# Early feed-forward weights, weight sums kept in DRAM, two-bank reads on ScalarE, and new instruction orders in a one-core transformer block

## The chip, the cores and the metric

The kernel runs on one core of one Trainium2 chip. A core has five engines with instruction streams of their own: TensorE (PE, with its weight loads listed as PEld), VectorE (DVE), ScalarE (ACT), GpSimd (POOL) and SyncE (SP), which here issues nearly all DMAs. The metric is the device time of one execution in microseconds, the median of several runs. Differences within about 1% can't be told from no change with this kernel.

## The reference

One transformer block on a sequence of 2048 tokens of width 512, in float32:

```
mod = silu(c) @ w_mod                      # six rows of 512: sa, ca, ga, sb, cb, gb
h   = layernorm(x) * (1 + ca) + sa
x   = x + ga * attention(h)
h   = layernorm(x) * (1 + cb) + sb
x   = x + gb * (relu(h @ w1 + b1)**2 @ w2 + b2)
```

The attention has 32 heads of width 16 and cuts the sequence into four segments of 512 tokens. Within a segment it is causal softmax attention; beside it each head reads a memory M, z that was summed over the segments before, with phi(t) = t + 1 for positive t and exp(t) otherwise:

```
for s in range(4):
    a_dot = softmax(q_s k_s^T / 4 + mask) v_s
    a_mem = phi(q_s) M / (phi(q_s) z + 1e-6)
    o_s   = g * a_mem + (1 - g) * a_dot      # g = sigmoid(beta), one per head
    M, z  = M + phi(k_s)^T v_s, z + sum(phi(k_s))
attention = concat(o_s) @ wo
```

The feed-forward layer is 512 to 1792 to 512 with a squared relu.

## The kernel before, in words

**Precision.** Matrix products that need float32 accuracy split each operand into a high part (a cast to a shorter float32 form) and a low part (the difference), and add three products. So each weight and each activation tile costs a cast, mostly on ScalarE, and a subtraction, mostly on VectorE.

**Stages.** A unit u is one segment (u // 4) and eight heads (u % 4); there are 16. For each unit, `qk` (L757) projects queries and keys into PSUM, ScalarE and VectorE split them into a staging tile `sg`, and twelve DMAs spread `sg` into four of the twelve slots of `ST` (`fill`, L812). `a_quad` (L863) forms scores a first time to get row maxima: TensorE at L870, maxima on VectorE at L875, a first pair of banks through a copy `ac` in SBUF (L908). The maxima go back into `ST` by DMA (L948). `b_quad` (L1032) forms the scores again with keys on the partitions (L1040), ScalarE takes the exponential (L1057), GpSimd zeroes what the mask forbids (L1044), and TensorE multiplies with the values (L1099). `vproj` (L823) projects the values, `mem` (L954) reads and updates the memory. `wo_tile` (L1222) applies wo to 128 tokens and adds x. The second layer norm and the feed-forward layer follow in four blocks of 512 tokens. Each block runs `ffn1` (L1434) seven times, q = 0 to 6, for 256 of the 1792 hidden features, and `ffn2` (L1493).

`ffn1` multiplies 2 x 2 blocks with seven products instead of eight. For that `load_w1` (L1382) makes, for each block and q, not only the four weight quarters but also four sums and differences of them (`sums`, L1404, four additions on VectorE), and splits all seven into high and low (casts at L1396, subtractions at L1399). The same sums are made again for each of the four blocks.

**Start.** x and the columns of w_mod for the first layer norm are loaded first. Matmuls without use (`N_WARM` of them, L546) keep TensorE busy from its start, reading a mask that GpSimd builds. `mod_parts` multiplies w_mod with silu(c) (L568), `mod_cols` turns the result into columns (L588), and the layer norm applies them after a transposition (L616). The first projection (`qk` of unit 0, L747) needs that and the split first columns of wq and wk. The load of wv goes into a buffer that the modulation weights of the start hold before it.

**Order.** `Plan` collects all operations as nodes with their dependences, buffers and a priority. For each engine a written list of node numbers (`ORDER`) says in which order it issues; numbers count the nodes in the order of their creation. The plan's constants (durations, `RARE`, `COLD`, `FREE`) model the engines' times; the written lists decide the order. An engine is a queue: an instruction that waits holds all behind it. SP's DMAs are issued in order too, at most eight in flight.

**Seam.** `open_ffn` (node `N_FFN`, L1371) closes the attention's SBUF buffers and opens those of the feed-forward layer: W2, w1r (raw w1, two), w1d (split w1, two), rr, r, u, gbb. `N_FFN` comes after all nodes of attention, and every load of w1 and w2 waits for it. The last four `wo_tile` calls, whose input stays in SBUF (X1L), lie behind it too.

**PSUM.** Each of the eight banks is a tile of its own (`bank`, L458), and each ScalarE read is of one bank.

Of the kernel before, what the change touches and what calls it, by code (L numbers as in the profile page):

```python
# [8 lines left out]
F32 = mybir.dt.float32  # L9
F32R = mybir.dt.float32r  # L10
# [8 lines left out]
P = 128  # L19
# [15 lines left out]
N_WARM = 70  # L35
# [35 lines left out]
1015 1106 926 1012 1018 1114 1022 1025 1002 928 1111 1142 930 1030 1034 1145 1120 1133 1038 1035-1036 1128 1045 1041
1272 1048 1363 1053 1364 1116 1365 1125 1234 1366 1242 1057-1059 1130 1148 1368 1155 1369 1151 1370 1135 1371 1163
1061 1253 1063 1167 1247 1396-1397 1239 1398-1399 1158 1266 1401-1402 1171 1403 1244 1404 1258 1168-1169 1178 1530
1181 1261 1531 1174 1532-1533 1263 1275 1186 1535-1536 1249 1537 1430 1438 1538 1468 1190-1192 1281 1413 1288 1414
1284 1415 1194 1416 1296 1196 1291 1418-1419 1268 1420 1449 1459 1443 1421 1278 1940-1941 1950-1951 1457 1435
1300-1302 1440 1304 1601 1311 1663 1314 1664 1454 1307 1665 1445 1666 1563 1471 1462 1668-1669 1319 1670 1464 1576
1671 1571 1474 1323 1582 1324-1325 1573 1796 1477 1797 1484 1798 1568 1492 1799 1487 1592 1801 1578 1802 1604 1590
1480 1803 1327 1804 1696 1329 1496 1595 1500 1497-1498 1607 1587 1507 1503 1734 1706 1510 1515 1519 1709 1610 1613
1520-1521 1617 1704 1597 1523 1620 1525 1737 1701 1625 1629 1740 1715 1633 1723 1630-1631 1640 1636 1958 1711 1959
1829 1842 1960 1834 1961 1867 1643 1963-1964 1648 1837 1965 1870 1966 1720 1652-1654 1873 1839 1743 1656 2114 1750  # L80
1658 2115-2116 1844 1728 2117 1987 1758 1988 1848 1989-1990 1725 2119 1746 1992-1993 1753 1861 1994-1995 1853
2120-2121 1730 1858 2122 2059 2021 1762-1764 1766 2034 2004 1856 2005 1769 2006 1773 2007 1776 1781 2009 2026 2010
# [1477 lines left out]
```

## Time and profile before

| | |
|---|---|
| median of 3 runs | 775.79 us (775.1 to 780.02) |
| profiled execution | 778.38 us, its span 776.7 us |
| TensorE clock granted, mean | 0.993 |
| busy: PE, PEld, DVE, ACT, POOL | 97%, 77%, 83%, 66%, 30% |
| read from HBM, written to it | 46.16 MB, 10.49 MB |
| attention's last unit ends, first ffn1 product | about 450 us, 460.46 us |

The page of the profile gives busy time per engine, the chain of work that ended last, the costliest groups of instructions and the DMA issues. Other views give the same execution by stretches of time, by wait, and in order of time. In a row of a group stand line, engine, operation, tiles out<-in, shapes and count, then busy time and the mean duration in ns, then the idle time before with what ended it. "x32" in a row in order of time merges neighbours of one line.

### The profile page before, as it was taken

How to read it: one execution, taken by the hardware profiler on the slowest of the kernel's cores; microseconds unless marked ns; L12 is line 12 of the kernel's file. 1: busy time of each engine (PE TensorE's matmuls, PEld its weight loads, DVE VectorE, ACT ScalarE, POOL GpSimd, SP SyncE). 2: the span in 40 equal slices, each digit the busy share in tenths (PEclk: the TensorE clock that was granted, in tenths of full speed). 3: DMA queues.
4: the chain of work that ended last, by engine and by line, in shares of the span. 5: the costliest groups of instructions: out<-in, count | busy, mean ns of one | idle time of the engine just before them, and what ended most of it. 6: DMA issues, size and time to landing. Idle time of an engine off the chain costs nothing.

```text
span 776.7 us, 17899 instructions
## 1 busy us (share of the span) xinstructions
PE 756.3 (97%) x6576; PEld 594.2 (77%) x6579; DVE 643.3 (83%) x1643; ACT 509.2 (66%) x990; POOL 233.6 (30%) x351
## 2 busy tenths in 40 slices
PE   8998999999999999999999989999999999999998
PEld 4777657675787858875676668888888888998896
DVE  3577877897888897789889889999989998998753
ACT  0658768879779896778756836667555665655541
POOL 3555453537665786534513310000000010000000
PEclk9999999999999999999999999999999999999999
DMA  7574661330443324244654166322351121043201
GB/s 270 174 182 107 203 182 52 89 98 23 118 124 83 98 71 103 55 116 127 167 176 132 49 201 192 96 82 82 108 174 58 41 96 55 28 136 101 63 1 54
DMA packets 78097, 84.81 MB, mean 109 GB/s; under 512 B 9014, under 2 KB 47674, under 8 KB 78011
## 3 DMA queue, kind: packets, MB, share of 16 engines
q1 hardware_dynamic: 77858, 83.55, 37.4%
q8 instruction: 52, 0.85, 0.5%
q14 instruction: 35, 0.28, 0.1%
q10 hardware_dynamic: 152, 0.13, 0.1%
HBM read 46.16 MB, written 10.49 MB: 73 GB/s over the span
## 4 chain that ended last, share of the span: by engine, by line
PE 69%; DVE 16%; ACT 6%; issue 3%; SPq 3%; DMA 2%; POOL 1%; ACTq 0%; DVEq 0%; POOLq 0%
PE bqk L757 9%; PE bpv L1099 6%; PE bpf L1502 5%; PE bpf L1504 5%; PE bpf L1503 5%; PE ba L870 5%; PE bpb L1040 5%; PE bv L837 4%; PE bhy L1443 3%; PE bhy L1444 2%; PE bhy L1445 2%; ACT pt L1057 2%; SPq L812 2%; PE bwarm L546 2%; DVE w1r L1404 2%
## 5 line engine op out<-in xcount | busy, mean ns | idle before, releaser
L875 DVE CUSTOM_DVE_ANT_0 ba<-ba,msk 128x128 f32<-128x128 f32 (+2 forms) x384 | 186.0, 542 | 33.9 <-PE ba L870 27.1
L1057 ACT ACTIVATE pt<-bpb 128x512 f32<-128x512 f32 x320 | 173.3, 616 | 31.2 <-PE bpb L1040 27.6
L1044 POOL TENSOR_SCALAR_AFFINE_SELECT pt<-pt 128x512 f32<-128x512 f32 x128 | 80.6, 649 | 93.4 <-ACT pt L1057 63.3
L1396 ACT CAST w1d<-w1r 128x768 fp32r<-128x768 f32 (+1 forms) x56 | 52.7, 944 | 76.5 <-PE bhy L1445 58.2
L757 PE MATMUL bqk<-HT,WQK 64*128 64x512 f32 x720 | 101.6, 396 | 0.0
L1502 PE MATMUL bpf<-W,rr 128*128 128x512 f32 x224 | 88.7, 396 | 0.0
L1504 PE MATMUL bpf<-W,rr 128*128 128x512 f32 x224 | 88.0, 393 | 0.0
L1503 PE MATMUL bpf<-W,rr 128*128 128x512 f32 x224 | 87.7, 391 | 0.0
L1099 PE MATMUL bpv<-pt,VT 128*32 128x512 f32 (+3 forms) x1024 | 81.3, 442 | 0.9 <-DVE mx L875 0.4
L1040 PE MATMUL bpb<-ST 64*128 64x256 f32 (+2 forms) x512 | 79.4, 350 | 2.3 <-ACT phi L803 0.4
L870 PE MATMUL ba<-ST 63*128 63x256 f32 (+2 forms) x512 | 75.1, 346 | 1.0 <-issue 0.4
L757 PEld LDWEIGHTS bqk<-HT,WQK 64*128 64x128 f32 x720 | 69.7, 186 | 8.2 <-issue 0.6
L1040 PEld LDWEIGHTS bpb<-ST 64*128 64x128 f32 x512 | 50.0, 185 | 21.2 <-ACT pt L1057 3.9
L870 PEld LDWEIGHTS ba<-ST 63*128 63x128 f32 x512 | 48.8, 187 | 19.4 <-issue 4.2
L1399 DVE TENSOR_TENSOR w1d<-w1r,w1d 128x768 fp32r<-128x768 f32 (+1 forms) x56 | 60.6, 1085 | 3.2 <-ACT w1d L1396 2.8
L1099 PEld LDWEIGHTS bpv<-pt,VT 128*32 128x32 f32 x1024 | 27.7, 110 | 38.1 <-issue 29.5
L837 PE MATMUL bv<-WVO,HT 64*128 64x512 f32 x384 | 54.9, 405 | 0.0
L875 DVE DVE_READ_ACCUMULATOR2_ANT mx<- 128x1 f32 x384 | 54.1, 141 | 0.0
L603 POOL TENSOR_SCALAR st_all<-st_all 128x4 f32<-128x4 f32 x4 | 1.8, 451 | 169.8 <-DVE st_all L596 169.8
L1404 DVE TENSOR_TENSOR w1r<-w1r 128x256 f32<-128x256 f32 x112 | 47.5, 424 | 3.2
L1481 ACT ACTIVATE r<-r,b1c 128x512 f32<-128x512 f32 x56 | 38.4, 719 | 17.8 <-DVE r L1463 17.5
L1504 PEld LDWEIGHTS bpf<-W,rr 128*128 128x128 f32 x224 | 42.0, 188 | 10.0 <-DVE rr L1489 0.3
(200 smaller groups left out, 1829.6 us busy)
## 6 DMA issues: line engine op xcount, KB each, us to landing
ST<-sg SPq DMA_DIRECT2D x192, 128.0 KB
w1r<-in_B_w SPq DMA_DIRECT2D x56, 256.0 KB
wm<-in_w_mod SPq DMA_DIRECT2D x24, 256.0 KB
xt<-in_A_x SPq DMA_DIRECT2D x16, 256.0 KB
xw<-in_A_x SPq DMA_DIRECT2D x16, 256.0 KB
wr<-in_B_w SPq DMA_DIRECT2D x14, 256.0 KB
o_dram<-on SPq DMA_DIRECT2D x12, 256.0 KB
ot<-o_dram SPq DMA_DIRECT2D x12, 256.0 KB
```

The costliest lines, as they stand in the source:

```text
L757: m = nc.tensor.matmul(bank(("qk", u, w)), W3(w, k, x, cc * P, (cc + 1) * P)[z], HT[z, y, k], start=(ph == 0 and k == 0 and i == 0), stop= ...
L837: m = nc.tensor.matmul(bank(("v", s, t)), HT[z, x, k, t * P:(t + 1) * P], WVO[z, k, y], start=(ph == 0 and k == 0 and i == 0), stop=(ph == ...
L870: nc.tensor.matmul(dst[:, c0:c0 + n], ST[b:b + 63, 0, sl, qt * P:(qt + 1) * P], ST[b:b + 63, 1, sl, :n], start=True, stop=True)
L875: nc.vector.tensor_tensor_reduce(i, i, msk[:, 512 - n:], scale=1.0, scalar=-3e38, op0=ALU.add, op1=ALU.max, accum_out=o)
L1040: nc.tensor.matmul(dst, ST[b:b + 64, 1, sl, kb * P:(kb + 1) * P], ST[b:b + 64, 0, sl, q0:512], start=True, stop=True)
L1044: nc.gpsimd.affine_select(out=ap, in_=ap, pattern=[[0, ap.shape[1]], [1, P]], compare_op=ALU.is_ge, fill=0.0, base=0, channel_multiplier=-1)
L1057: ns = [act(512, lambda j=j: nc.scalar.activation(buf("PPP"[n], pt)[:, i + j], bank(keys[j]), AF.Exp, scale=0.25), pr[slot] + 0.01 + 0.001 ...
L1099: nc.tensor.matmul(bank(o)[32 * hq:32 * hq + 32, q0:q0 + src.shape[1]], v[:, a:a + 32], src, start=start, stop=stop, tile_position=(0, 32 ...
L1404: nc.vector.tensor_tensor(r[:, o], r[:, a], r[:, b], op=f)
L1502: nc.tensor.matmul(p, rh, FF["W2"][:, f, 0], start=(f == 0), stop=False)
L1503: nc.tensor.matmul(p, rh, FF["W2"][:, f, 1], start=False, stop=False)
L1504: nc.tensor.matmul(p, rl, FF["W2"][:, f, 0], start=False, stop=(f == NF - 1))
```

## The change

- **Buffers.** `ST` (48 KB per partition), `sg` and `ac` become constant tiles that outlive attention. The feed-forward layer's w1r lies in `sg`, w1d in slots 4 to 11 of `ST`, rr and the last oT in slots 0 to 3, gbb in a rest of slot 11, r in `ac`, u in the x buffers.
- **Early w1.** The loads of the first two groups (block 0, q = 0 and 1) wait no longer for `N_FFN` but for the last unit's reads of `sg`; their first casts wait for the B scores of units 13 and 14, whose slots of `ST` they take. b1 is loaded from `N_LATE` on. w2 and gbb still wait for `N_FFN`.
- **Sums in DRAM.** In block 0 the four sums of each q are made as before and then stored to DRAM (`s_dram`). Blocks 1 to 3 load the three raw quarters that are used directly, and the sums from DRAM, into the two raw buffers one after the other.
- **PSUM.** One tile of eight banks; a bank is a slice of it. Where two banks were read by two ScalarE instructions, one reads both with a stepped slice: exponentials, ac, VT, mt, pk. The plan gives a pair its banks in ascending order.
- **Start.** 46 warm matmuls for 70, reading a tile that VectorE clears first.
- **Orders.** All five lists are new. The plan's constants change with them (`RARE`, `FREE`, `START`, the duration of the GpSimd power and of the sums, the size of the first loads).

```diff
-N_WARM = 70
+N_WARM = 46
 ORDER = {
     "PE": """
-16 67 26 82 79 74 73 31 37 75 53 27 40 28 78 35 39 50 63 81 17 29 76 54 33 68 65 85 51 83 24 45 3 58 47 77 61 25 32 19
-84 52 55 43 42 66 38 126 23 48 18 41 114 127 59 62 49 115 56 60 103 95 69 105 97 36 70 80 20 64 22 34 46 71 30 169-170
...
+16-17 32 21 61 51 25 54 49 38 26 29 47 45 36 3 23 31 59 42 53 37 46 60 28 57 33 19 56 79 55 44 48 40 81 50 71 90-91 73
+102 20 18 103 41 30 34 39 58 22 52 35 24 43 27 155 145-147 156 148-149 157-158 150-151 159 152 160-162 287-290 181-184
...
     "SP": """
-89 87 90 88 102 91 99 101 100 92-94 146-147 136-137 157 156 166 739 742 13 740-741 194 203 197-198 201 196 193 202 200
...
+77 76 63 75 66 65 78 64 67-70 122 112 123 113 132-133 142 647-648 650 649 174 178 172 171 176 169-170 177 173 180 175
...
-    RARE, COLD, NEAR, LATE, RING = 2.3, 3.4, 0.12, 0.1, 8
+    RARE, COLD, NEAR, LATE, RING = 1.8, 3.4, 0.12, 0.1, 8
+    START = 5.8
-    FREE = {"PE": 2.0, "ACT": 2.6, "DVE": 2.7, "POOL": 2.4, "SP": 0.8, "NIL": 0.0}
+    FREE = {"PE": 1.2, "ACT": 2.6, "DVE": 2.7, "POOL": 2.4, "SP": 0.8, "NIL": 0.0}
...
+        two = [key for pool, key in n.get if pool[0] == "#"]
+        if len(two) == 2 and self.slot[two[0]] > self.slot[two[1]]:
+            a, b = two
+            self.held[a][-1], self.held[b][-1] = self.held[b][-1], self.held[a][-1]
+            self.slot[a], self.slot[b] = self.slot[b], self.slot[a]
...
+    s_dram = [dram.tile([P, 8 * P], F32, name=f"s_dram{q}") for q in range(NF // 2)]
+    wz = const.tile([P, P], BF, name="wz")
+    nc.vector.memset(wz, 0.0)
-    ST = sb.tile([P, 2, NSLOT, 512], F32R, name="ST")
+    ST = const.tile([P, 2, NSLOT, 512], F32R, name="ST")
+    SG = const.tile([P, 4, 512], F32R, name="SG")
+    AC = const.tile([P, 2, 512], F32, name="AC")
...
+    PB = ps.tile([P, 8, 512], F32, name="PB")
     def bank(key):
-        if key not in TL:
-            TL[key] = ps.tile([P, 512], F32, name=f"b{key[0]}", tag=f"bank{PL.slot[key]}")
-        return TL[key]
+        return PB[:, PL.slot[key]]
+    def banks(keys):
+        a, b = (PL.slot[k] for k in keys)
+        return PB[:, a:b + 1:b - a]
...
-            ns = [act(512, lambda j=j: nc.scalar.activation(buf("PPP"[n], pt)[:, i + j], bank(keys[j]), AF.Exp, scale=0.25),
-                      pr[slot] + 0.01 + 0.001 * j, after=[k], put=[keys[j]]) for j in (0, 1)]
+            ns = [act(1024, lambda: nc.scalar.activation(buf("PPP"[n], pt)[:, i:i + 2], banks(keys), AF.Exp, scale=0.25),
+                      pr[slot] + 0.01, after=[k], put=keys)]
...
-    n_b1 = sp(lambda: nc.sync.dma_start(b1c, b1.rearrange("(f p) -> p f", p=P)), z - 2.8, 1 << 14, after=[N_FFN])
+    n_b1 = sp(lambda: nc.sync.dma_start(b1c, b1.rearrange("(f p) -> p f", p=P)), z - 2.8, 1 << 14, after=[N_LATE])
...
+    late = NU - 1
+    SGU = [n for n in PL.nodes if ("sg", late) in n.put]
     def load_w1(s, q, pr):
...
-        n = sp(load, pr - 0.2, 1 << 19, 2, after=[N_FFN], get=[("w1r", kr)])
-        h = act(768, lambda: hi(1, 4, 0), pr, sbuf=True, after=[n], get=[("w1d", kd)])
-        l = dve(768, lambda: lo(1, 4, 0), pr + 0.01, after=[h])
-        n = op("DVE", 1.36, sums, pr + 0.02, after=[l])
-        h2_ = act(1024, lambda: hi(0, 4, 3), pr + 0.03, sbuf=True, after=[n])
-        l2_ = dve(1024, lambda: lo(0, 4, 3), pr + 0.04, after=[h2_], put=[kr])
+        first = s == 0 and q < 2
+        ks = kr if s == 0 else ("w1s", s, q)
+        n = sp(lambda: load(s), pr - 0.2, 1 << 19 if s == 0 else 3 << 17, 2, after=SGU if first else [], get=[("w1r", kr)])
+        h = act(768, lambda: hi(kr, 1, 4, 0), pr, sbuf=True, after=[n, *([z for pp in range(4) for z in STU[4 * (NU - 3 + q) + pp]] if first else []),
+                                                                    W1N[0, 0][0][0] if first and q else None], get=[("w1d", kd)])
+        l = dve(768, lambda: lo(kr, 1, 4, 0), pr + 0.01, after=[h], put=[kr] if s else [])
+        if s == 0:
+            n = op("DVE", 1.8, sums, pr + 0.02, after=[l])
+            W1S[q] = sp(lambda: nc.sync.dma_start(s_dram[q], raw(kr).rearrange("p b k n -> p (b k n)")), pr + 0.3, 1 << 19, after=[n], put=[kr])
+        else:
+            n = sp(lambda: nc.sync.dma_start(raw(ks).rearrange("p b k n -> p (b k n)"), s_dram[q]), pr - 0.1, 1 << 19, after=[W1S[q], n], get=[("w1r", ks)])
+        h2_ = act(1024, lambda: hi(ks, 0, 4, 3), pr + 0.03, sbuf=True, after=[n, h])
+        l2_ = dve(1024, lambda: lo(ks, 0, 4, 3), pr + 0.04, after=[h2_], put=[ks])
```

In the lists before, 16 to 85 are the warm matmuls, 87 to 90 the loads of x, 91 to 94 and 99 to 102 those of the modulation weights for scale and shift, 95 and 103 their matmuls, 97 and 105 their columns, 114, 115, 126 and 127 the transposes of the first layer norm. In the new lists all of these are smaller by 24.

More of the change, by code (lines that the diff above doesn't have):

```diff
@@ L545, in block_kernel @@
     for i in range(N_WARM):
-        pe("F", 0.22, lambda: nc.tensor.matmul(bank(wk_), msk[:, :P], msk, start=True, stop=True), 50.0,
+        pe("F", 0.22, lambda: nc.tensor.matmul(bank(wk_).rearrange("p (a n) -> p a n", a=4), wz, wz[:, None, :].to_broadcast([P, 4, P]), start=True, stop=True), 50.0,
            get=[("bank", wk_)] if i == 0 else (), put=[wk_], after=[n_w0] if i else ())
@@ L561, in mod_parts @@
         loads = [sp(lambda k=k: nc.sync.dma_start(row(k), wmod[k * P:(k + 1) * P, m * D:(m + 1) * D]),
-                    pr + 0.001 * k, 1 << 18, get=[at[k]] if at[k] else (), after=after) for k in range(KD)]
+                    pr + 0.001 * k, 1 << 18 if after else 175000, get=[at[k]] if at[k] else (), after=after) for k in range(KD)]
         b = ("mod", m)
@@ L596, in ln_stats @@
         nc.vector.bn_aggr(mv, bs)
-    mhalf = const.tile([P, 4], F32)
+    mhalf = const.tile([P, 4], F32, name="mhalf")
     MHN = op("POOL", 0.1, lambda: nc.gpsimd.memset(mhalf, -0.5), -5.0)
@@ L679, in ln1 @@
                 st[t].left += 1
[L680 removed]
+        r = op("POOL", 1.25, lambda: ln_rstd(TL[mv], 4), p_stat + 0.05, after=[*st, MHN])
         HTN[s] = []
@@ L907, in a_quad @@
                    get=[("#A", k) for k in keys] + [("mx", mx), ("ac", ac)])
-        cp = [act(512, lambda j=j: nc.scalar.copy(buf("ac", ac)[:, j], bank(keys[j])), pr[0] + 0.01 + 0.001 * j, after=[first],
-                  put=[keys[j]]) for j in (0, 1)]
+        cp = [act(1024, lambda: nc.scalar.copy(buf("ac", ac), banks(keys)), pr[0] + 0.01, after=[first], put=keys)]
         def acv():
@@ L939, in turn_m @@
                 z = slice(64 * r, 64 * r + 64)
-                nc.tensor.transpose(bank(b[r])[:16, z], TL[mx][z], ident[z, z])
+                nc.tensor.transpose(bank(b[r])[:16, 0:64], TL[mx][z], ident[z, z])
         n = pe("R", 0.06, turn_m, p_tail, after=reds, get=[("#D", k) for k in b], put=[mx])
-        n = [act(64, lambda r=r: nc.scalar.mul(buf("mt", mt, F32R)[:, 64 * r:64 * r + 64], bank(b[r])[:16, 64 * r:64 * r + 64], -1.0),
-                 p_tail, after=[n], get=() if r else [("mt", mt)], put=[b[r]]) for r in (0, 1)]
+        n = [act(128, lambda: nc.scalar.mul(buf("mt", mt, F32R).rearrange("p (r n) -> p r n", r=2), banks(b)[:16, :, 0:64], -1.0),
+                 p_tail, after=[n], get=[("mt", mt)], put=b)]
         sl = (4 * u + 2 * qd) % NSLOT
@@ L1267, in ln2 @@
     def ln2(s, pr, wait=()):
-        r = op("POOL", 0.5, lambda: ln_rstd(st_all[:, 4 * s:4 * s + 4], 4), pr[0] - 0.1, after=[X1N[4 * s + t] for t in range(4)] + (XWN if s else []))
+        r = op("POOL", 1.25, lambda: ln_rstd(st_all[:, 4 * s:4 * s + 4], 4), pr[0] - 0.1, after=[X1N[4 * s + t] for t in range(4)] + (XWN if s else []))
         H2N[s] = [None] * 7
@@ L1380, in wraw, with raw, load @@
         return TL[k]
+    W1S = {}
+    halves = lambda t: t.rearrange("p (a n) -> p a n", a=2)
+    late = NU - 1
+    SGU = [n for n in PL.nodes if ("sg", late) in n.put]
+    ACU = [n for n in PL.nodes if ("ac", late, 0) in n.put or ("ac", late, 1) in n.put]
     def load_w1(s, q, pr):
         kr, kd = ("w1r", s, q), ("w1d", s, q)
-        def load():
-            TL[kr] = FF["sb"].tile([P, 4, 2, P], F32, name="w1r", tag=f"w1r{PL.slot[kr]}")
+        def raw(k):
+            if k not in TL:
+                TL[k] = SG.bitcast(F32)[:, 2 * PL.slot[k]:2 * PL.slot[k] + 2].rearrange("p a (b k n) -> p (a b) k n", b=2, k=2)
+            return TL[k]
+        def load(n0=0):
@@ L1429, in block_kernel @@
            get=[("xr", kb)], after=[X1N[4 * NS - 1]])
-    n_b2 = dve(512, lambda: nc.vector.tensor_tensor(gab, TL[kb], FF["gbb"], op=ALU.mult), z + 0.4, after=[n, n_gbb], put=[kb])
+    n_b2 = dve(512, lambda: nc.vector.tensor_tensor(halves(gab), halves(TL[kb]), FF["gbb"], op=ALU.mult), z + 0.4, after=[n, n_gbb], put=[kb])
     F1, F2 = {}, {}
+    STZ = [z for pp in range(4) for z in STU[4 * late + pp]]
     OUTN = []
```

350 lines of the change are left out of this document (167 added, 183 removed), and 15 rows, old and new, of the table ORDER.

## The prediction

> **What bounds the kernel now.** I read the page first, then the table of busy time by stretches, then the start and the seam between attention and feed-forward in order of time, then the groups and waits that the edit touches.
>
> The page (span, part 1, chain of part 4):
> ```profile
> span 776.7 us, 17899 instructions
> ...
> PE 756.3 (97%) x6576; PEld 594.2 (77%) x6579; DVE 643.3 (83%) x1643; ACT 509.2 (66%) x990; POOL 233.6 (30%) x351
> ...
> PE 69%; DVE 16%; ACT 6%; issue 3%; SPq 3%; DMA 2%; POOL 1%; ACTq 0%; DVEq 0%; POOLq 0%
> ```
> TensorE is the spine, yet the last-ending chain leaves it for 31% of the span. So the gain to look for is in stretches where TensorE waits, and they differ by stage. The stretches (us; busy of PE, PEld, DVE, ACT, POOL with instruction counts; then granted clock, DMA share, GB/s):
> ```profile
> core 0: us, PE busy (x) PEld busy (x) DVE busy (x) ACT busy (x) POOL busy (x), PEclk, DMA share, GB/s
> 60.00:250.00 190.00, 185.21 (x2152) 134.09 (x2154) 156.11 (x531) 153.04 (x360) 106.31 (x154) 0.98 0.40 109
> 250.00:440.00 190.00, 187.68 (x1984) 133.81 (x1983) 164.04 (x526) 143.88 (x320) 90.09 (x138) 1.00 0.41 113
> ...
> 400.00:420.00 20.00, 20.00 (x156) 13.87 (x156) 18.05 (x51) 12.14 (x27) 5.69 (x10) 1.00 0.53 152
> 420.00:440.00 20.00, 19.68 (x170) 12.54 (x167) 17.29 (x40) 15.45 (x33) 5.46 (x8) 1.00 0.29 94
> ...
> 440.00:450.30 10.30, 10.03 (x95) 6.46 (x93) 9.92 (x24) 5.71 (x12) 2.83 (x5) 1.00 0.15 53
> 450.30:460.50 10.20, 7.30 (x33) 5.61 (x31) 8.22 (x19) 2.96 (x4) 3.01 (x4) 0.83 0.83 231
> 460.50:580.00 119.50, 118.01 (x741) 104.11 (x740) 116.52 (x201) 72.97 (x103) 0.00 (x0) 1.00 0.40 122
> 580.00:740.00 160.00, 159.97 (x1008) 143.61 (x1007) 140.33 (x236) 92.36 (x124) 2.15 (x2) 1.00 0.25 75
> ```
> Four readings. In attention (60 to 440) TensorE has no matmul in flight for 4.8 + 2.3 us, and 2% of the clock is missing in its first half. At the seam (450.3 to 460.5) it idles 2.9 us and has 0.83 of the clock. From 460.5 to 580 VectorE is 97.5% busy: there it is a second bound. From 580 on TensorE never pauses; that last part can't get shorter by anything in this change.
>
> Matmuls overlap, so I compare weight loads per time where the mix is the same: 143.61/160 = 0.898 after 580, 104.11/119.5 = 0.871 before it. The missing 0.027 is worth 119.5 x 0.0264/0.898 = 3.5 us. The Trainium skill (Perfetto Trace Analysis, "Identifying the Most-Contended Engine") says matmul busy time is a poor measure of headroom and weight-load share a good one; by the matmul column alone this stretch would hide only 119.5 - 118.0 = 1.5 us, and the sum below would be 2 us smaller.
>
> **The start.** In order of time:
> ```profile
> 2.66 4.41 SPq L561 DMA_DIRECT2D wm<-in_w_mod  x8
> 3.27 8.83 PE L546 MATMUL bwarm<-msk 128*128 128x512 bf16 x32 [3.27 <-POOL msk L439]
> 6.04 0.69 DVE L595 BATCH_NORM_STATS2 bs<-xt 128x6 f32<-128x512 f32 x1 [0.64 <-DMA xt<-in_A_x]
> 8.94 1.05 POOL L604 TENSOR_TENSOR mv<-mv,mhalf 128x4 f32<-128x4 f32 x1
> 10.02 1.92 DVE L607 TENSOR_SCALAR xt<-xt,mv 128x512 f32<-128x512 f32 x4 [1.49 <-POOL mv L604]
> 12.18 3.19 PE L546 MATMUL bwarm<-msk 128*128 128x512 bf16 x14
> 19.00 1.92 PE L568 MATMUL bmod<-wm,cs 128*32 128x512 f32 x16
> 20.20 1.33 SPq L701 DMA_DIRECT2D w<-in_A_wv  x2
> 25.52 0.38 PE L747 MATMUL bqk<-HT,WQK 128*128 128x256 f32 x1 [0.42 <-ACT HT L636]
> ```
> ```profile
> 2.00:4.00 2.00, 0.73 (x2) 0.26 (x2) 1.65 (x4) 0.96 (x2) 1.90 (x10) 1.00 0.96 307
> 0.00:8.40 8.40, 5.13 (x16) 2.11 (x17) 5.24 (x13) 1.59 (x2) 5.61 (x23) 1.00 0.76 252
> 0.00:11.20 11.20, 7.93 (x29) 3.38 (x30) 6.55 (x16) 1.59 (x2) 6.88 (x25) 1.00 0.83 285
> 0.00:12.60 12.60, 9.33 (x35) 3.92 (x36) 7.29 (x17) 1.75 (x3) 6.88 (x25) 1.00 0.86 295
> 17.00:20.20 3.20, 3.20 (x27) 1.65 (x28) 0.00 (x0) 0.00 (x0) 0.00 (x0) 1.00 0.03 8
> ```
> The bytes: 252 GB/s x 8.4 us = 2.1 MB, 285 x 11.2 = 3.2 MB, 295 x 12.6 = 3.7 MB. x and both sets of modulation weights (1.05 MB each) were therefore in by 11.2 us, but their matmuls ran at 19.00, because TensorE's list puts 46 warm matmuls and the layer-norm transposes ahead of them. From the first of them to the first projection pass 25.52 - 19.00 = 6.5 us. And between 17.0 and 20.2 the DMA engines are idle: the load of wv waits for the buffer that those matmuls read.
>
> The new lists (numbers are places in the list of operations; 24 warm ones less shift them by 24) put 28 warm matmuls, the modulation matmul of shift (79), 4 warm, its columns (81), 1 warm, that of scale (71), two transposes (90-91), columns (73), two transposes (102, 103), 2 + 11 warm, projection (155). On SP the shift's weights go between the tiles of x, and the first columns of wq right after those of wk. Worked out:
> - Completion: at 307 GB/s x was in by about 5.3 us by bytes, and a statistic that waited for it began at 6.04: I add 0.7 us to arrivals.
> - Scale's weights 11.2 + 0.7 = 11.9; then the same 6.5 us less one of the two matmul groups (1.92/2): 17.4 us.
> - x, now among other loads, 8.4 + 0.7 = 9.1; one statistic 0.69, rstd and its wait 1.5, four normalizations 1.9: 13.2, before the projection needs it.
> - First columns of wk and wq 12.6 + 0.7 = 13.3, then two casts and subtractions beside the above.
> - Warm work: the first 28 at 8.83/32 = 0.28 us take 7.7 us, from an earlier start (their operand no longer comes from GpSimd's mask at 3.27), so they end near 9 us; the 13 last at 3.19/14 = 0.23 take 3.0.
>
> The first projection comes at 17.5 instead of 25.5. The whole chain of attention hangs on it, as does the load of wv, whose gap closes. I take 7.5 us; the 24 removed warm matmuls alone are 24 x 0.23 = 5.5. Zero if a later wait binds; an idle stretch among the fewer warm ones could cost a slow clock:
> ```profile
> 61.00:64.50 3.50, 3.23 (x23) 3.23 (x25) 2.55 (x6) 2.13 (x7) 0.00 (x0) 0.57 0.11 18
> ```
> that is 3.5 x 0.43 = 1.5 us each time.
>
> **The seam and the first feed-forward block.** In order of time:
> ```profile
> 450.55 0.99 SPq L1390 DMA_DIRECT2D w1r<-in_B_w  x2
> 453.40 0.78 PE L1241 MATMUL bwot<-ident,X1L 128*128 128x128 f32 x5 [2.60 <-DVE X1L L1170]
> 455.40 0.83 ACT L1396 CAST w1d<-w1r 128x768 fp32r<-128x768 f32 x1 [0.49 <-DMA w1r<-in_B_w]
> 460.46 0.37 PE L1443 MATMUL bhx<-H2a,w1d 128*128 128x256 f32 x1
> ```
> ```profile
> L1399 DVE TENSOR_TENSOR w1d<-w1r,w1d 128x768 fp32r<-128x768 f32 (+1 forms) x56 | 60.6, 1085 | 3.2 <-ACT w1d L1396 2.8 <-ACT u L1456 0.3
> L1404 DVE TENSOR_TENSOR w1r<-w1r 128x256 f32<-128x256 f32 x112 | 47.5, 424 | 3.2
> ```
> Today no w1 load starts before attention is over (450.55); the first product follows 10 us later, and TensorE meanwhile waits 2.6 us for VectorE's last normalization. After the edit two w1 groups are loaded and split as soon as the last unit's staging and the score slots of units 13 and 14 are free, so products can fill that gap and the clock stays up. Available: 2.9 us idle, 0.17 x 10.2 = 1.7 us of clock, 3.5 us in 460.5 to 580: 8.1 us.
>
> What VectorE allows: one group is two subtractions (2 x 1.085) and four sums (4 x 0.424), 3.9 us; two are 7.7 us, moved into 400 to 450.3, where it has 1.95 + 2.71 + 0.38 = 5.0 us free. So 2.7 us of it delays the normalizations there or stays late. Against that, sums of blocks 1 to 3 go altogether (21 x 1.7 us), of which some four lie before 580 (a block takes about 80 us, half of 580 to 740, so the second begins near 540, and 40/11.4 is 3.5 groups): 6.8 us off the stretch where VectorE is 97.5% busy. After 580 TensorE covers the rest and it is worth nothing. I take 5.5 of the 8.1 us; below nothing if the moved splits hold up the last units, down to -2.7.
>
> New transfers: 7 stores of 0.5 MB, 21 loads of 0.5 MB, and 0.375 for 0.5 MB raw, about 12 MB more, into stretches with a DMA share of 0.25 to 0.40; hidden. The store waits on SP for the sums, and W2, xh and further w1 loads queue behind it; a block needs a new group each (740 - 580)/14 = 11.4 us, and the later chain (cast 0.83, subtraction 1.1, twice, and two transfers) fits. Uncovered it would be some 1 us per group.
>
> **ScalarE on two banks.**
> ```profile
> L1057 ACT ACTIVATE pt<-bpb 128x512 f32<-128x512 f32 x320 | 173.3, 616 | 31.2 <-PE bpb L1040 27.6 <-PE ba L870 1.7 <-POOL pt L1044 0.8
> L1487 ACT ACTIVATE r<-r 128x1024 f32<-128x1024 f32 x28 | 29.7, 1061 | 0.8
> ...
> PEld bpb L1040 <- ACT pt L1057: 3.9, 13, 0.4
> ...
> PEld ba L870 <- ACT pt L1057: 2.8, 7, 0.9
> ```
> 320 x 616 ns would be 197 us, yet the engine is busy 173.3: neighbours already overlap. 160 wide ones at 1061 ns (an SBUF row, the nearest) are 169.8: 3.5 us off an engine that holds 6% of the chain. The Trainium skill (ScalarE: Activation LUTs, "What ACT_TABLE_LOAD costs") gives 186 ns + 0.833 ns per element and an overlap of 93 ns back to back; by it a merged pair saves 93 ns, 15 us in all, and the trace's overlap agrees in kind (24/320 = 74 ns). Against the gain, the first bank of a pair comes free 1.06 - 0.62 = 0.44 us later; 20 waits of that sort cost at most 8.8 us. Copies to ac, VT, pk and mt change alike and are smaller. I take 1 us gain. bias loads, rows in other tiles, the planner's new constants (it follows written lists): nothing.
>
> **Sum.** The profiled execution took 778.38 us (span 776.7 and 1.7 around it), 2.6 above the median of 775.79. 778.4 - 7.5 - 5.5 - 1 = 764.4; on the median's footing **762 us**, 1.8% faster.
>
> **The rivals.**
> - More than that: the new lists also remove attention's idle 7.1 us and the lost 2% x 190 = 3.8 us of clock. For: ScalarE and VectorE are only 76 to 86% busy there, so there is room. Against: a list can't remove a dependence. 762 - 10 = 752 us. Chance 0.13.
> - One of the two main gains is absent: the new start finds another late arrival (x behind the modulation weights), or VectorE's moved splits delay attention by what the seam gains. 767.5 to 770 us, within 1%. For: only 5.0 us free for 7.7. Chance 0.22.
> - Slower: all banks become one tile, and a read of banks a and b is a strided slice. If the waits are drawn for the whole stretch, TensorE's writes to banks between wait for reads that don't touch them. Price: the waits above average 3.9/13 = 0.3 us; at every second of 160 exponentials 80 x 0.3 = 24 us, 786 us. 47 such waits eat the gain, 73 make it slower by 1%. For: today's waits are few because each bank is a tile. Against: the slice names its step. Chance 0.14.
> - That the change doesn't do what it says, the lists stalling on w1 buffers not free as early as planned, gives the second case's time.
>
> **The numbers.** The forecast has 0.51, its own range 753 to 768. Changes within 1% (768 to 783.5) can't be told from none here. Faster: 0.51 + 0.13 = 0.64; same 0.22; slower 0.14. The range 748 to 780 leaves out the third rival and the tail below the first.
>
> **What would show it.** First projection near 17 to 18 us; no DMA gap before wv; first w1 load before 440 us and first product before 455; clock 1.0 at the seam; VectorE under 92% in the 120 us behind the seam; weight loads there near 0.89; some 160 exponentials of about 1.05 us; waits of TensorE on ScalarE no longer than today. Waits on exponentials of many more than 20 would mean the third rival; a first projection after 22 us, or attention as long as before plus 3 us, the second.

## The result and the profile after

The changed kernel takes 982.92 us (median of four runs, 981.24 to 984.55); the kernel before, beside it on the same chip, 775.44 us. The ratio is 1.266, 95% interval 1.260 to 1.272: 207 us slower, where the forecast was 14 us faster. The profiled execution took 981.31 us. Two single executions in the experiments below stand far off (897.99 us with own tiles, 4027.02 us with neighbouring banks); the medians given there include them, the ratios leave them out.

The page of the changed kernel (span, part 1, the granted clock and the chain; of part 5 the two costliest groups):

```profile
span 979.6 us, 17529 instructions
...
PE 831.5 (85%) x6555; PEld 612.4 (63%) x6555; DVE 619.8 (63%) x1560; ACT 503.7 (51%) x722; POOL 233.9 (24%) x351
...
PEclk9987699988699799687998989999999999999999
...
PE 38%; DVE 5%; ACT 5%; issue 2%; DMA 0%; ACTq 0%; DVEq 0%; SPq 0%
...
L878 DVE CUSTOM_DVE_ANT_0 PB<-PB,msk 128x128 f32<-128x128 f32 (+2 forms) x384 | 187.6, 541 | 181.7 <-PE PB L873 102.6
L1058 ACT ACTIVATE pt<-PB 128x1024 f32<-128x1024 f32 x160 | 161.7, 1023 | 143.6 <-PE PB L1041 39.3
```

VectorE and ScalarE have no more work than before, and yet each stands still for more than 140 us ahead of its largest group. In the kernel before, ScalarE stood still for 31.2 us ahead of the exponentials, and VectorE for 33.9 us ahead of the maxima:

```profile
L875 DVE CUSTOM_DVE_ANT_0 ba<-ba,msk 128x128 f32<-128x128 f32 (+2 forms) x384 | 186.0, 542 | 33.9 <-PE ba L870 27.1
```

The span is 202.9 us longer, and on TensorE that splits in two: without a matmul in flight it was 776.7 - 756.3 = 20.4 us before and is 979.6 - 831.5 = 148.1 us now (+127.7); its busy time grew by 831.5 - 756.3 = 75.2 us for the same matmuls less the 24 warm ones. The clock falls to 0.6 again and again in the first two thirds; its mean is 0.920 instead of 0.993, which as an estimate makes 831.5 x 0.080 - 756.3 x 0.007 = 61 us of the 75.

The stretches show that it all lies in attention (us; busy PE, PEld, DVE, ACT, POOL with counts; then granted clock, DMA share, GB/s):

```profile
60.00:655.00 595.00, 458.42 (x4190) 291.08 (x4187) 334.72 (x1078) 298.21 (x426) 198.94 (x295) 0.87 0.27 73
655.00:680.00 25.00, 22.04 (x138) 18.45 (x137) 23.98 (x48) 11.56 (x18) 3.10 (x5) 0.93 0.64 210
680.00:800.00 120.00, 119.93 (x762) 107.66 (x761) 107.87 (x177) 76.22 (x108) 2.17 (x2) 1.00 0.48 152
800.00:960.00 160.00, 159.65 (x1009) 143.82 (x1008) 111.94 (x166) 87.38 (x118) 0.00 (x0) 1.00 0.32 102
```

Attention from 60 us on took about 390 us and now takes 595, with TensorE busy for 77% of it at 0.87 of its clock. From 680 us on the feed-forward layer is what the prediction described: weight loads at 107.66/120 = 0.897, VectorE at 90% and then 70%. The start also did its part (in order of time):

```profile
11.50 1.91 SPq L705 DMA_DIRECT2D w<-in_A_wv  x2
13.37 1.06 PE L572 MATMUL PB<-wm,cs 128*32 128x512 f32 x8
19.66 0.47 PE L751 MATMUL PB<-HT,WQK 128*128 128x256 f32 x1
```

The first projection is at 19.66 us instead of 25.52, and wv is loaded from 11.50 us on instead of 20.20.

What attention waits for (engine, line and what was waited for; us in total, times, longest):

```profile
DVE PB L878 <- ACT pt L1058: 40.0, 24, 7.3
ACT pt L1058 <- PE PB L1041: 39.3, 39, 5.9
ACT pt L1058 <- DVE mx L878: 30.9, 18, 3.4
ACT pt L1058 <- PE PB L761: 28.3, 15, 4.5
PEld PB L1041 <- ACT pt L1058: 26.4, 25, 2.2
PEld PB L761 <- ACT pt L1058: 18.2, 14, 2.3
PE PB L1041 <- ACT pt L1058: 17.2, 21, 2.0
```

L1058 is the exponential. It reads B scores that L1041 writes. L761 writes the projections of queries and keys, and L878 takes the maxima of A scores. Some such waits are due, since banks pass from one user to the next. But before, TensorE's two largest rows on the exponential held 13 and 7 short waits, and now waits run in both directions between all that touches PSUM. In order of time it is seen that most are not due:

```profile
195.57 0.39 PE L841 MATMUL PB<-WVO,HT 64*128 64x512 f32 x1
...
200.95 1.02 ACT L1058 ACTIVATE pt<-PB 128x1024 f32<-128x1024 f32 x1 [2.65 <-DVE mx L878]
202.03 0.97 PE L841 MATMUL PB<-WVO,HT 64*128 64x512 f32 x5 [1.40 <-ACT pt L1058]
203.27 1.02 ACT L1058 ACTIVATE pt<-PB 128x1024 f32<-128x1024 f32 x1 [1.29 <-PE PB L873]
204.34 0.50 PE L1041 MATMUL PB<-ST 64*128 64x256 f32 x3 [1.11 <-ACT pt L1058]
205.87 1.02 ACT L1058 ACTIVATE pt<-PB 128x1024 f32<-128x1024 f32 x1 [1.58 <-PE PB L841]
206.92 0.70 DVE L878 CUSTOM_DVE_ANT_0 PB<-PB,msk 128x512 f32<-128x512 f32 x1 [3.10 <-ACT pt L1058]
206.95 1.65 PE L841 MATMUL PB<-WVO,HT 64*128 64x512 f32 x6 [0.91 <-ACT pt L1058]
...
213.69 0.38 ACT L833 COPY VT<-PB 128x256 f32<-128x256 f32 x1
```

L841 is the value projection. One group of it writes the same two banks from 195.57 until they are copied to VT at 213.69, so no exponential of this stretch can read them. And yet it stops for the exponential that ends at 201.97 and goes on at 202.03; the exponential of 205.87 waits for L841; and behind that VectorE and TensorE start again at 206.92 and 206.95. The engines take turns.

The built program says why. It lists what each instruction waits for, so the banks that an instruction uses can be put beside those of the read that it waits for. Of the waits of TensorE on reads of two banks, 64 are for a bank that is read, and 167 for a bank that lies between the two; VectorE has 27 and 81 (by up to five more, depending on how they are counted). None is for a bank outside that stretch. Of the 268 pairs only 53 got neighbouring banks; 215 step over one to six others.

### The profile page after: what moved, and what is told of

The parts are those of the page before. It is cut to its first block, busy times and chain, and to the rows that moved or that the text cites. A ratio compares the mean times of both kernels' runs of the same rounds, so it can differ in the third digit from the quotient of the medians.

```text
span 979.6 us, 17529 instructions
## 1 busy us (share of the span) xinstructions
PE 831.5 (85%) x6555; PEld 612.4 (63%) x6555; DVE 619.8 (63%) x1560; ACT 503.7 (51%) x722; POOL 233.9 (24%) x351
## 4 chain that ended last, share of the span: by engine, by line
PE 38%; DVE 5%; ACT 5%; issue 2%; DMA 0%; ACTq 0%; DVEq 0%; SPq 0%
PE PB L1523 5%; PE PB L1525 5%; PE PB L1524 5%; PE PB L1462 4%; PE PB L1463 4%; PE PB L1464 4%; ACT pt L1058 3%; PE PB L1100 3%; PE PB L1215 2%; PE PB L1217 1%; PE PB L1041 1%; PE PB L1216 1%; PE PB L873 1%; DVE PB L878 1%; PE PB L1242 1%
## 5 line engine op out<-in xcount | busy, mean ns | idle before, releaser
L878 DVE CUSTOM_DVE_ANT_0 PB<-PB,msk 128x128 f32<-128x128 f32 (+2 forms) x384 | 187.6, 541 | 181.7 <-PE PB L873 102.6
L1058 ACT ACTIVATE pt<-PB 128x1024 f32<-128x1024 f32 x160 | 161.7, 1023 | 143.6 <-PE PB L1041 39.3
L761 PE MATMUL PB<-HT,WQK 64*128 64x512 f32 x720 | 128.6, 454 | 20.9 <-ACT pt L1058 13.0
L1100 PE MATMUL PB<-pt,VT 128*32 128x512 f32 (+3 forms) x1024 | 95.0, 494 | 26.9 <-ACT pt L1058 11.9
L873 PE MATMUL PB<-ST 63*128 63x256 f32 (+2 forms) x512 | 87.0, 386 | 25.8 <-ACT pt L1058 12.8
L1041 PE MATMUL PB<-ST 64*128 64x256 f32 (+2 forms) x512 | 89.5, 390 | 21.2 <-ACT pt L1058 17.2
L761 PEld LDWEIGHTS PB<-HT,WQK 64*128 64x128 f32 x720 | 78.9, 215 | 42.0 <-ACT pt L1058 18.2
L1523 PE MATMUL PB<-W,ST 128*128 128x512 f32 x224 | 88.6, 396 | 0.0
L1525 PE MATMUL PB<-W,ST 128*128 128x512 f32 x224 | 87.9, 392 | 0.0
L1524 PE MATMUL PB<-W,ST 128*128 128x512 f32 x224 | 87.6, 391 | 0.0
L1041 PEld LDWEIGHTS PB<-ST 64*128 64x128 f32 x512 | 55.0, 210 | 49.0 <-ACT pt L1058 26.4
L841 PE MATMUL PB<-WVO,HT 64*128 64x512 f32 x384 | 57.4, 412 | 11.0 <-ACT pt L1058 9.4
L1410 DVE TENSOR_TENSOR ST<-SG,ST 128x768 fp32r<-128x768 f32 (+1 forms) x56 | 60.2, 1085 | 8.7 <-ACT ST L1407 8.7
L1462 PE MATMUL PB<-H2a,ST 128*128 128x256 f32 x196 | 55.9, 285 | 0.1
L1463 PE MATMUL PB<-H2a,ST 128*128 128x256 f32 x196 | 55.2, 282 | 0.0
L1464 PE MATMUL PB<-H2a,ST 128*128 128x256 f32 x196 | 55.0, 281 | 0.0
L878 DVE DVE_READ_ACCUMULATOR2_ANT mx<- 128x1 f32 x384 | 54.1, 141 | 0.0
```

Source lines behind the costliest of these rows:

```text
L761: m = nc.tensor.matmul(bank(("qk", u, w)), W3(w, k, x, cc * P, (cc + 1) * P)[z], HT[z, y, k], start=(ph == 0 and k == 0 and i == 0), stop= ...
L873: nc.tensor.matmul(dst[:, c0:c0 + n], ST[b:b + 63, 0, sl, qt * P:(qt + 1) * P], ST[b:b + 63, 1, sl, :n], start=True, stop=True)
L878: nc.vector.tensor_tensor_reduce(i, i, msk[:, 512 - n:], scale=1.0, scalar=-3e38, op0=ALU.add, op1=ALU.max, accum_out=o)
L1041: nc.tensor.matmul(dst, ST[b:b + 64, 1, sl, kb * P:(kb + 1) * P], ST[b:b + 64, 0, sl, q0:512], start=True, stop=True)
L1058: ns = [act(1024, lambda: nc.scalar.activation(buf("PPP"[n], pt)[:, i:i + 2], banks(keys), AF.Exp, scale=0.25), pr[slot] + 0.01, after=[k] ...
L1100: nc.tensor.matmul(bank(o)[32 * hq:32 * hq + 32, q0:q0 + src.shape[1]], v[:, a:a + 32], src, start=start, stop=stop, tile_position=(0, 32 ...
```

## The experiments

**Theory (the stretch):** the stepped slice `PB[:, a:b+1:b-a]` is taken as everything from bank a to bank b, and engines wait for the banks between. **Rivals:** the new lists or the buffers made constant starve TensorE; or the wide read itself does, because a bank comes back 0.4 us later.

### Own tiles, one bank per read

```diff
-    PB = ps.tile([P, 8, 512], F32, name="PB")
     def bank(key):
-        return PB[:, PL.slot[key]]
+        if key not in TL:
+            TL[key] = ps.tile([P, 512], F32, name=f"b{key[0]}", tag=f"bank{PL.slot[key]}")
+        return TL[key]
...
-            ns = [act(1024, lambda: nc.scalar.activation(buf("PPP"[n], pt)[:, i:i + 2], banks(keys), AF.Exp, scale=0.25),
+            ns = [act(1024, lambda: [nc.scalar.activation(buf("PPP"[n], pt)[:, i + j], bank(keys[j]), AF.Exp, scale=0.25) for j in (0, 1)],
```

(and the copies to ac, VT, mt and pk alike)

> The changed kernel, with each bank a tile of its own again and two one-bank reads wherever it had one stepped read of two banks. Lists, early w1, sums in DRAM, buffers and start are those of the change. Theory (the stretch): the stepped slice makes TensorE, VectorE and ScalarE wait for banks that lie between the two that are read, and nothing else in the change is slow: 755 to 770 us, no 40 us of attention with TensorE busy for less than 37, and waits of TensorE and VectorE on the exponentials back to some 20 in all. Rival (the lists or the buffers): the new orders, or ST, SG and AC as constant tiles, are what starves TensorE: 950 us or more. Rival (the wide read): a bank is given back 0.4 us later because ScalarE reads two at once; that is gone here too, so this run does not tell it from the stretch, the one with neighbouring banks does.

Measured: 766.4 us, ratio to the kernel before 0.986 (0.983 to 0.989). The lists and buffers are not to blame: with them and without the stepped reads the kernel is 1.4% faster than before. TensorE is busy for at least 38.29 us of every 40 in attention. The waits of TensorE and VectorE on exponentials are 51 over all rows, 18.0 us, not the some 20 expected; the kernel before has 37 by the same count, 14.5 us, and the changed one 219. Its page and stretches:

```profile
span 765.5 us, 17894 instructions
...
PE 753.5 (98%) x6555; PEld 596.2 (78%) x6555; DVE 613.1 (80%) x1560; ACT 507.0 (66%) x990; POOL 233.7 (31%) x351
```

```profile
60.00:250.00 190.00, 187.57 (x2210) 135.71 (x2210) 157.91 (x543) 151.71 (x353) 107.84 (x158) 0.98 0.40 107
250.00:440.00 190.00, 188.10 (x1922) 131.12 (x1914) 164.07 (x514) 142.47 (x314) 89.22 (x137) 0.99 0.43 117
440.00:450.30 10.30, 8.15 (x51) 5.70 (x44) 9.89 (x23) 2.70 (x4) 3.09 (x5) 0.77 0.59 180
450.30:460.50 10.20, 10.20 (x63) 9.20 (x62) 9.27 (x18) 3.74 (x7) 0.00 (x0) 0.90 0.67 206
460.50:580.00 119.50, 119.40 (x764) 107.72 (x764) 109.31 (x181) 76.63 (x109) 0.00 (x0) 1.00 0.51 160
```

### One tile, one bank per read

The tile of eight banks stays; only the stepped reads go (the last two lines of the diff above, and the copies).

> The changed kernel with the one PSUM tile of eight banks kept and only the stepped reads replaced by two one-bank reads each. If the one tile itself ties the banks together, this stays near 980 us; if only the stepped slice does, it equals the kernel with own tiles within 1% (755 to 770 us).

Measured: 766.6 us, 0.988 (0.984 to 0.992), as own tiles. The one tile costs nothing; reads of one bank are told apart within it.

### The PSUM part alone, in the kernel before

```diff
+    PB = ps.tile([P, 8, 512], F32, name="PB")
...
-            ns = [act(512, lambda j=j: nc.scalar.activation(buf("PPP"[n], pt)[:, i + j], bank(keys[j]), AF.Exp, scale=0.25),
+            ns = [act(512, lambda j=j: once(keys[0], lambda: nc.scalar.activation(buf("PPP"[n], pt)[:, i:i + 2], banks(keys), AF.Exp, scale=0.25)),
```

(`once` issues at the first of the two nodes and nothing at the second; ac, VT, mt, pk alike)

> The kernel before with only the PSUM part of the change: one tile of eight banks and each of the 268 pairs read by one stepped instruction at the place of the first of the two in ScalarE's list; lists, w1 and start as before. The stretch: 775 + 160 to 240 us, so 935 to 1015 us. If the lists or the buffers of the change were to blame: 775 us, give or take 2%.

Measured: 981.9 us, a single run. Old lists with stepped reads are as slow as new lists with them.

### Wide reads with nothing between

```diff
+        pair = sum(pool[0] == "#" for pool, _ in n.get) == 2
+        if pair:
+            free = self.pools["bank"]
+            near = [(a, a + 1) for a in free if a + 1 in free]
+            if near:
+                ab = min(near, key=lambda z: max(free.index(z[0]), free.index(z[1])))
+                self.pools["bank"] = [*ab, *(z for z in free if z not in ab)]
...
-        return PB[:, a:b + 1:b - a]
+        return PB[:, a:b + 1] if b - a == 1 else None
```

(a pair that gets no neighbours is read by two instructions of one bank)

> The changed kernel with the one tile and wide reads, but the plan gives a pair two neighbouring banks when two are free (178 of the 268 pairs get them and are read by one ScalarE instruction; the other 90 by two one-bank reads). No wide read has a bank between its two. The stretch: 750 to 772 us, as the kernel with own tiles, give or take 1% for the wide reads. The wide read as such: with two thirds of the pairs still wide, two thirds of the loss stay, 900 to 920 us.

Measured: 765.6 us, 0.985 (0.982 to 0.988). 178 wide reads, no loss: the wide read itself is not the cause. Nor is there a gain over one bank per read (766.6): the wide read is worth nothing that can be measured here.

### Three doses between none and all

Exponentials alone stepped; copies alone stepped; and the plan of the last experiment with all pairs stepped, so that the number of wide reads is the change's and only the banks differ.

> The changed kernel with stepped two-bank reads for the 160 exponentials alone; the copies to ac, VT, mt and pk read one bank each. By the price of the prediction's third rival (80 waits of 0.3 us) 766 + 24 = 790 us. By the price that the whole change shows, 983 - 766 = 217 us over the 248 waits for banks between (167 of TensorE and 81 of VectorE in the built program), 0.87 us each, with 103 + 59 such waits here: 766 + 141 = 907 us.

> The changed kernel with the exponentials reading one bank each and stepped two-bank reads for the 108 copies alone (ac, VT, mt, pk). Waits for banks between in the built program: 64 of TensorE and 29 of VectorE. At 0.875 us each: 766 + 81 = 847 us. If what costs is the length of the exponentials' reads (1.02 us) and the shorter copies hold nothing up: under 800 us.

> The changed kernel, every pair read by one stepped instruction as in the change, but with the plan that gives a pair neighbouring banks when two are free: 178 pairs have nothing between them, 90 are stepped over others. As many wide reads as in the change; waits for banks between are 61 of TensorE and 26 of VectorE. At 0.875 us each: 766 + 76 = 842 us. If the reading of two banks as such were the cost: 983 us, as the change.

Measured, one run of each of the three, with all kernels in one table (waits for banks between are those of TensorE and of VectorE in the built program; the loss is against 766 us, for the old lists against 776):

| kernel | wide reads over other banks | waits for banks between | us | loss | us per wait |
|---|---|---|---|---|---|
| one bank per read; neighbours only | 0 | 0 | 766 | 0 | |
| all wide, neighbours where free | 90 | 61 + 26 | 852.4 | 86 | 0.99 |
| copies stepped | 90 | 64 + 29 | 835.7 | 70 | 0.75 |
| exponentials stepped | 125 | 103 + 59 | 909.5 | 143 | 0.88 |
| old lists, all stepped | 201 | 144 + 81 | 981.9 | 206 | 0.92 |
| the change | 215 | 167 + 81 | 982.9 | 217 | 0.88 |

The loss follows the number of waits, not the number of wide reads: all 268 wide lose 86 us when most are neighbours and 217 when few are. It lies between 0.75 and 0.99 us per wait, so the forecasts made from 0.87 (907, 847 and 842 us) are met within 11 us; why it differs by kind stays open.

### The new start alone, in the kernel before

46 warm matmuls on the cleared tile and the change's first instructions on each list.

```diff
-N_WARM = 70
+N_WARM = 46
...
-        pe("F", 0.22, lambda: nc.tensor.matmul(bank(wk_), msk[:, :P], msk, start=True, stop=True), 50.0,
+        pe("F", 0.22, lambda: nc.tensor.matmul(bank(wk_).rearrange("p (a n) -> p a n", a=4), wz, wz[:, None, :].to_broadcast([P, 4, P]), start=True, stop=True), 50.0,
```

> The kernel before with only the new start: 46 warm matmuls that read a cleared tile, and the change's order of the first instructions on each engine (up to the first projections); all behind it as before. Theory: the first projection comes some 6.7 us earlier, as it does with own tiles (18.86 for 25.52 us), and all of attention moves with it: 768 to 770 us, ratio 0.991. Rival: a later arrival (the second tiles of x, wv, the other columns of wq and wk) takes it back within the first 60 us: 774 to 777 us.

Measured: 769.7 us, 0.990 (0.988 to 0.992), 8.0 us less than the 777.7 of the kernel before beside it. The start's gain is kept to the end. But it is not all there at the first projection, which comes at 19.57 us, 6.0 earlier than before; the value projection starts 7.5 us earlier (28.4 instead of 35.9), and the last unit's product with the values is 7.7 earlier (439.5 instead of 447.2).

### Own tiles with late w1

```diff
-        n = sp(lambda: load(s), pr - 0.2, 1 << 19 if s == 0 else 3 << 17, 2, after=SGU if first else [], get=[("w1r", kr)])
+        n = sp(lambda: load(s), pr - 0.2, 1 << 19 if s == 0 else 3 << 17, 2, after=[*SGU, N_FFN] if first else [], get=[("w1r", kr)])
```

(and all that depends on these loads moved behind attention in each list)

> The kernel with own tiles, but the first two w1 groups wait for the end of attention again, and all that hangs on them goes behind attention's last instruction in each list. If the early products are worth what the prediction says of the seam (4.6 of its 8.1 us): 768 to 771 us. If not, since with own tiles TensorE still idles 2.2 us there and the clock still falls: 764 to 767 us.

Measured: 770.1 us, 0.991 (0.989 to 0.993): 3.7 us (0.5%) more than with early w1, though the intervals touch, so that this worth is not clear of noise. In order of time, TensorE now waits 5.5 us for the first cast:

```profile
447.71 0.58 PE L1461 MATMUL bhx<-H2a,ST 128*128 128x256 f32 x1 [5.50 <-ACT ST L1404]
```

### Own tiles with VectorE's sums given back

```diff
-            r = raw(kr)
+            r = raw(ks)
...
-        l2_ = dve(1024, lambda: lo(ks, 0, 4, 3), pr + 0.04, after=[h2_], put=[ks])
+        l2_ = dve(1024, lambda: (lo(ks, 0, 4, 3), sums() if s else None), pr + 0.04, after=[h2_], put=[ks])
```

> The kernel with own tiles, in which VectorE makes the four sums of each weight group in blocks 1 to 3 again, in a buffer that has been read for the last time (they are used by nobody; the sums from DRAM are still used). That is 21 x 4 x 0.424 = 35.6 us more on VectorE, of which some four groups, 6.8 us, before 580 us. If VectorE was the second bound there: 767 to 770 us and the share of weight loads in the 120 us behind the seam falls back to 0.87. If not: 764 to 767 us and 0.90.

Measured: 787.1 us, ratio to before 1.012 (1.009 to 1.014), 20 us more than own tiles: beyond what either case expected. From 460 to 500 us nothing changes (weight loads 36.19 of 40 us, as with own tiles); the loss comes behind it, in this stretch among others (busy PE, PEld, DVE, ACT, POOL, then the clock):

```profile
540.00:580.00 40.00, 34.99 (x210) 30.63 (x211) 33.01 (x57) 19.36 (x25) 0.00 (x0) 0.96 0.39 127
```

Here TensorE is idle for 5.0 us while VectorE is only 83% busy. The weight loads' share from 460.5 to 580 falls to 100.27/119.5 = 0.84, and from 580 to 700 TensorE is busy for 113.2 us instead of the 120.0 with own tiles. The additions hold up what stands behind them in VectorE's order, in stretches where the busy share shows room. In order of time:

```profile
550.74 1.80 DVE L1412 TENSOR_TENSOR SG<-SG 128x256 f32<-128x256 f32 x4
552.46 0.68 DVE L1480 TENSOR_TENSOR AC<-AC,bhy 128x512 f32<-128x512 f32 x1
...
553.28 0.47 PE L1520 MATMUL bpf<-W,ST 128*128 128x512 f32 x1 [1.60 <-DVE AC L1480]
```

From 500 to 740 us TensorE waits for VectorE for 12.9 us, with own tiles for 0.4. The sums also keep the buffers longer, and the loads then wait for them; that is not what costs, since ScalarE's casts wait for loads for 0.7 us in that stretch, with own tiles for 0.3. The new lists need the shorter VectorE; how much the sums in DRAM gained against the old lists can't be read from this run, because in the kernel before TensorE is busy for 39.54 of the 40 us from 540 with the sums in place.

### The seam: keep the clock, then relieve VectorE

With own tiles the first w1 is loaded at 383.31 and the first product comes at 442.93, as predicted (before 440 and before 455), but the seam is no better:

```profile
446.11 1.33 PE L1239 MATMUL bwot<-ident,X1L 128*128 128x128 f32 x5 [1.88 <-DVE X1L L1168]
```

```profile
445.00:446.00 1.00, 0.00 (x0) 0.78 0.63 75
446.00:447.00 1.00, 0.89 (x4) 0.50 1.05 352
...
451.00:452.00 1.00, 1.00 (x4) 0.50 0.99 373
452.00:453.00 1.00, 1.00 (x7) 0.80 0.42 162
```

These are the wait in order of time, and then stretches of one microsecond (busy PE, clock, DMA share, GB/s). One wait of 1.88 us for the last normalization, and the clock is at half for over six microseconds: 6 x 0.50 + 0.20 = 3.2 us of clock lost behind a wait of 1.9, 3.4 with the 0.22 of the wait's own last microsecond.

```diff
         def tr():
+            if last and "full" not in FF:
+                FF["full"] = True
+                for i in range(8):
+                    nc.tensor.matmul(bank(b).rearrange("p (a n) -> p a n", a=4), wz, wz[:, None, :].to_broadcast([P, 4, P]), start=True, stop=True)
             for k in range(KD):
```

> The kernel with own tiles and eight warm matmuls more, at the seam, ahead of the transposes of the first of the last four products with wo (the fourth of them waits 1.9 us for VectorE's last normalization, and behind it the granted clock is at 0.5 for some 6.5 us). The fillers take 8 x 0.22 = 1.8 us of that wait. If the clock falls because of the wait: it stays at 1.0 there, 766 - 3.4 = 762 to 763 us. If it falls for another reason (the stretch of small matmuls and copies before): no change, 766 us, or 1 to 2 us more.

Measured: 767.3 us, 0.989 (0.985 to 0.992). The clock holds, and nothing is gained. Stretches of two microseconds (as above, busy PE first), what TensorE waits for in them, and VectorE's share (third busy time) of the whole seam:

```profile
444.00:446.00 2.00, 2.00 (x13) 1.00 0.82 174
446.00:448.00 2.00, 1.62 (x11) 1.00 0.96 260
448.00:450.00 2.00, 1.43 (x6) 1.00 0.61 241
```

```profile
447.78 0.50 PE L1212 MATMUL bwop<-WVO,ST 128*128 128x512 f32 x1 [0.24 <-ACT ST L1248]
449.08 0.51 PE L1214 MATMUL bwop<-WVO,ST 128*128 128x512 f32 x1 [0.57 <-DVE ST L1250]
```

```profile
440.00:460.00 20.00, 18.78 (x136) 14.57 (x129) 19.45 (x40) 6.29 (x10) 3.10 (x5) 1.00 0.66 183
```

At full speed TensorE reaches the next operands before they are split, and VectorE is busy for 19.45 of these 20 us. So the sums of the first two groups went to GpSimd:

```diff
-                nc.vector.tensor_tensor(r[:, o], r[:, a], r[:, b], op=f)
+                (nc.gpsimd if s == 0 and q < 2 else nc.vector).tensor_tensor(r[:, o], r[:, a], r[:, b], op=f)
```

> The kernel with own tiles and the eight fillers at the seam, and the four sums of the first two weight groups (1.8 us each on VectorE, directly ahead of the subtraction that the first product with wo waits for) made by GpSimd, which is idle there; at half of its 1.29 us for 128x512 they take some 2.6 us a group. If VectorE is what the seam waits for once the clock holds: 3.4 us of clock less some 1 us of GpSimd's longer sums, 763 to 764 us, ratio to the kernel before 0.983. If something else is late next: 766 to 767 us.

Measured: 766.9 us, 0.986 (0.983 to 0.989). No gain that can be told, though the 0.983 of the first case lies at the interval's edge. VectorE is now busy for 17.11 of the 20 us; GpSimd's four sums took 3.15 and 4.82 us, and one product on VectorE beside them (L1435) took 1.22 us instead of 0.69. What would shorten the seam stays open.

## Why the prediction was wrong, and where it was right

**The step that failed** is the third rival's price and chance, and with it the term "I take 1 us gain" for two banks per read. The mechanism was named: waits drawn for the whole stretch. Its price was 80 waits of 0.3 us, 24 us; the runs show 217 us, from 766 to 982.9. The sign given for it came: over all rows of TensorE and VectorE there are 219 waits on exponentials, where the kernel before has 37. Three things were mis-sized:

- Their number. Only the exponentials were counted, and only TensorE. In the built program 248 waits are for banks between, 81 of them VectorE's. The copies count too: 70 us by themselves, beside 143 for the exponentials.
- The price of one. 0.3 us was the mean of one row of the trace before, in which such waits are rare. In the same row (weight loads of the B scores) it is now 26.4/25 = 1.06 us, and it works both ways: the wide read waits for the writers and readers of the banks between (143.6 us of idle ahead of the exponentials instead of 31.2), so that in attention the engines take turns.
- The clock. The granted clock is 0.87 over the 595 us in which TensorE now waits so often, and was 0.98 and 1.00 in the two halves of attention before; the price of the third rival left this out. Busy time grew by 75 of the 203 us, by the estimate above 61 of them through the clock.

The chance of 0.14 leaned on "the slice names its step". That is how the slice is written; no row of the trace of before could tell how waits are drawn for it. The nearest bound in that trace was not today's waits but the length of the reads themselves: 160 x 1.06 us for the exponentials alone, 170 us, if each shuts the other engines out. This is an estimate made afterwards; the exponentials alone cost 143.

On what the chip itself needs, the Trainium skill (PSUM — Partial Sum Buffer, "PSUM bank collisions raise a hardware error") says that engines on different banks run side by side without a collision and that semaphores should guard bank by bank. By that rule the 248 waits protect nothing. The kernels that read one bank, or two neighbours, agree: they run without these waits at 766 us.

**The start:** right in size, and in part by luck. 7.5 us were predicted for 8.0 measured alone, and the gap ahead of wv closed. But the first projection was to come at 17.5 us, 8 earlier, and came at 19.57, 6.0 earlier: in the changed kernel scale's matmul is at 13.37 instead of 11.9, and the projection 6.3 us behind it instead of 5.5. The rest of the gain arose behind the first projection, where none was forecast; why stays open.

**The seam and first block:** 5.5 us were predicted; early w1 alone is worth some 3.7. The available 8.1 us were three pieces. Weight loads from 460.5 to 580 rose from 0.871 to 107.72/119.5 = 0.901, worth 4.0 us where 3.5 were available, with VectorE at 109.31/119.5 = 91.5%. Most of that is not early w1's: with late w1 the share is 106.97/119.5 = 0.895. At the seam early w1 makes up for what the new lists would otherwise lose there (from 440 to 460 TensorE is busy for 17.85 us, with late w1 for 14.03), but against the kernel before nothing is gained: 2.9 us of idle and 1.7 of clock became 2.15 and 10.3 x 0.23 + 10.2 x 0.10 = 3.4: 0.9 us worse. "Products can fill that gap and the clock stays up" was wrong: they filled the time before the wait, and VectorE, not the load of w1, decides when the wait ends. The prediction had that number (5.0 us free for 7.7 of moved splits) and took only 8.1 - 5.5 = 2.6 us off for it.

**ScalarE:** an exponential takes 1023 ns (1061 estimated) and the engine is busy with them for 161.7 us (169.8 estimated). Worth: nothing that can be measured, since with neighbours the kernel is no faster than with single reads.

**The sum:** without the stepped reads 766 us stand against 762, and the gain of 14 us was 10. Attention's idle time and the new lists brought the first rival little: the two stretches from 60 to 440 have 4.3 us idle for 7.1, but 5.7 us of clock lost for 3.8 (from clocks given in hundredths, so each to about 2 us).

## What to carry to other kernels

A slice with a step may be tracked as all that lies between its ends: in a tile that several engines share, read two banks at once only where they are neighbours (and let the allocator make them so), or give each bank its own tile. When a change alters how dependences are expressed, count the waits in the built program by the bank they are really for; a trace of the old kernel can't show them. Price a new wait by the longest instruction it can meet, in both directions and with the clock that it costs, not by the mean of the waits that exist.

## What was not expected of the hardware

One wait of 1.88 us (444.23 to 446.11, with own tiles) was enough for TensorE's granted clock to fall to half. In steps of 0.2 us it is 0.92 from 445.4, 0.50 from 445.6 and 1.00 again from 452.4: it falls within the wait and stays low for 6.8 us. The Trainium skill (TensorE: Matmul & The Clock Gate, "HAM oscillation — how this bites in real kernels") asks for no idle gap above about 3.4 us; this trace has the fall in a shorter one. And eight matmuls without use kept the clock at 1.00, yet the time stayed (767.3 us instead of 766.4): there the slow clock cost nothing that can be measured. VectorE is busy for 19.45 of 20 us there, but taking sums off it did not shorten the kernel either.
